# Retention and a leaky-ReLU MLP on one core: half of the loads of blocks 2 to 11 on SyncE's queue, and a new order of the opening

## The chip, the cores and the metric

The kernel runs on one core of a Trainium2 chip. A core has five engines, each with its own in-order instruction queue: TensorE (PE, matrix products; its weight loads are listed as PEld), VectorE (DVE), ScalarE (ACT), GpSimd (POOL) and SyncE (SP). Here GpSimd and SyncE only issue DMA transfers. The metric is device time in microseconds; the time before is the median of three runs.

## The reference

Per batch and head, retention with a decay that depends on the head, then a two-layer MLP over all heads together:

```
scores = q k^T / sqrt(64);  ret = (scores * Dmat) v      # Dmat[i, j] = gamma_h^(i-j) for i >= j, else 0
x      = ret, heads side by side                         # 4608 tokens x 512
out    = leaky_relu(x @ w_in, 0.01) @ w_out              # w_in 512 x 2048, w_out 2048 x 512
```

q, k and v are 8 batches x 8 heads x 576 tokens x 64, float32; inside, the kernel computes in fp16 with float32 sums.

## The kernel before

**Blocks and groups.** The 4608 tokens are 36 blocks of 128 (two chunks of 64), four blocks make a group of 512 tokens. Per block the retention part runs, with the decay folded into q, k and v and a running state per head; the MLP runs per group. Its first layer is plain for groups 0 and 1; from group 2 on, and for all second layers, it is a seven-product scheme (Strassen-like) with sums on VectorE.

**Jobs.** Each piece of work is a job with a name, and one string, `ORDER`, lists all jobs in the sequence in which they are emitted. So each engine's queue holds its jobs in the sequence of that string, and waits (semaphores) follow from the data. A table `ENGINE` says which of VectorE and ScalarE does a job that either could do. `CFG["loads"]` says which queue issues each load. The jobs that matter here, for block u and group g:

| job | engine | what it does |
|---|---|---|
| `ldu.0`, `ldu.1`, `ldu.2` | POOL or SP | load q, k, v of block u, 256 KB each, into a float32 buffer t_0, t_1 or t_2; there are four buffers of each (128 KB halves where a block spans two batches) |
| `cqu`, `cku`, `cvu` | DVE or ACT | cast q, k, v to fp16 (q and v scaled); this frees the load's buffer |
| `tpu.x`, `ytu.x` | PE, DVE/ACT | transpose q (x=0) or k (x=1) on TensorE (line 411) and copy the result; from block 8 on `tru`, a DMA transpose on SyncE |
| `sbu` | PE | state products k^T v (line 454); needs cku and cvu |
| `stu.j`, `sxu` | DVE, ACT | add the state of chunk j (lines 485 to 491), cast it |
| `sau`, `mku` | PE, DVE | scores and mask (lines 445, 460) |
| `oau` or `cau`, `owu`; `xu` | PE; ACT/DVE | output products (line 542), copy into xT |
| `wif`, `woc` | POOL | load a quarter of w_in, w_out, cast to fp16 on the way |
| `hg.f.t`, `lg.f.t` | PE, ACT | plain first layer: feature tile f, tokens from t (line 640), and its leaky ReLU |
| `+n` | PE | n idle matrix products (filler, line 980) while TensorE has no data |

h0.4 to h0.7 need w_in quarter 1, h0.8 to h0.11 quarter 2, h0.12 to h0.15 quarter 3, h0.0 to h0.3 quarter 0. In the text, q3, k3, v3 stand for the loads of block 3, wi1 for w_in quarter 1.

The load itself and where a state product gets its waits:

```
def run(t=t, x=x, c=c, parts=parts, eng=eng):          # line 346
    for j, rows in parts:
        b, w = (c + j) // CB, (c + j) % CB
        engine[eng].dma_start(
            out=t[CH * j : CH * j + rows],
            in_=(q, k, v)[x][b, :, CH * w : CH * w + rows, :].rearrange("h t d -> t h d"),
        )
...
jb = add(
    f"sb{u}", "PE", sb, [cast[u, 1], cast[u, 2]] + states.get(u - 1, []), [], [qk16[u], v16[u], sc_banks],
    mode="q",
)
```

**What sets the order around the change.** Three things: each queue is issued in its own sequence; a load waits until the cast that last read its buffer is done; and each queue has eight semaphore lanes used in turn, so a DMA also waits until the eighth before it on the same kind of queue (GpSimd's, or SyncE's and ScalarE's together) has landed. Buffers are given out in the sequence in which loads appear in `ORDER`.

Of the kernel before, what the change touches and what calls it, by code (L numbers as in the profile page):

```python
# [33 lines left out]
class Plan:  # L34
# [52 lines left out]
    for eng, names in {  # L87
        "DVE": """
            ck0 cq0 sx0.0 yt0.0 cq1 sx0.1 cv1 cq2 sx1.0 yt2.1 ck3 cq3 yt3.1 cv3 sx2.1 yt3.0 cq4 cv4 x3 ck5 cq5
            cv5 yt5.1 cq6 sx5 cv6 cq7 ck7 cv7 yt7.0 b0.cA cv8 ck10 sx8.0 cv9 cq9 cq11 cq12 cv10 b1.cA cv13 ck15  # L90
            cv14 cq14 cv15 cq15 sx13.1 sx14 cq16 cv16 cv17 cq17 cq18 a2.3.k5 sx17.0 cv18 sx18 cq19 a3.1.u2 x17
            cv20 ck21 cq21 sx19 a3.2.k5 cq22 cv22 sx20 ck23 cv23 cq23 x20 cv24 cq25 sx23 a4.2.cA cv25 a4.2.u2
            cq26 cq27 cv27 sx25 a5.0.u2 a5.0.k5 cq28 cq29 cv29 ck30 cq30 cv30 ck31 cv31 cq32 sx30 cq33 ck33
            a6.0.cA cv33 cv34 ck34 cq35 cq34 a6.2.cA b5.u2 cv35 a6.3.u2 x32 a7.0.cA x33 a7.0.k5 b5.21 a7.1.cA
            b6.11 b6.u2 a7.3.cA a7.3.u2 a8.0.k5 b7.k5 a8.2.u2 a8.2.k5 b7.21 a8.3.u2 b8.21
        """,
        "ACT": """
            cv0 yt0.1 x0 ck1 ck2 yt1.1 yt1.0 cv2 yt2.0 x1 sx1.1 sx2.0 x2 sx3.0 ck4 sx3.1 yt4.1 yt4.0 ck6 sx4.1
            x4 yt5.0 x5 yt6.0 yt6.1 sx6 yt7.1 sx7 x7 x6 ck8 b0.11 cq8 ck9 b0.u2 cq10 b0.k5 cv11 ck12 sx9 x8 ck11
            cv12 sx10 cq13 b0.21 x9 ck13 sx11 b1.11 sx12 x10 b1.u2 x11 ck14 a2.0.cA b1.k5 a2.0.u2 a2.0.k5 x12  # L100
            a2.1.cA a2.1.u2 x13 a2.1.k5 ck16 ck17 sx15 a2.2.cA a2.2.u2 b1.21 a2.2.k5 sx16 x14 a2.3.cA x15
            a2.3.u2 ck18 b2.cA a3.0.cA b2.11 a3.0.u2 a3.0.k5 a3.1.cA cv19 b2.u2 x16 a3.1.k5 ck19 b2.k5 a3.2.cA
            ck20 cq20 a3.2.u2 cv21 b2.21 ck22 x18 a3.3.cA a3.3.u2 a3.3.k5 x19 b3.cA a4.0.cA b3.11 sx21 ck24
            a4.0.u2 a4.0.k5 cq24 a4.1.cA a4.1.u2 sx22.1 a4.1.k5 x21 b3.u2 ck25 b3.k5 ck26 sx24 a4.2.k5 x22 cv26
            a4.3.cA x23 a4.3.u2 a4.3.k5 ck27 b3.21 a5.0.cA b4.cA ck28 cv28 sx26.0 b4.11 x24 ck29 a5.1.cA a5.1.u2
            a5.1.k5 x25 sx27 sx28 b4.u2 a5.2.cA x26 sx29 b4.k5 a5.2.u2 a5.2.k5 x27 a5.3.cA ck32 a5.3.u2 cv32
            a5.3.k5 cq31 b4.21 x28 x29 sx31.1 a6.0.u2 a6.0.k5 sx32 b5.cA a6.1.cA b5.11 a6.1.u2 x30 a6.1.k5 x31
            a6.2.u2 a6.2.k5 sx33 b5.k5 ck35 a6.3.cA a6.3.k5 sx34 sx35.0 a7.0.u2 b6.cA a7.1.u2 a7.1.k5 a7.2.cA
            a7.2.u2 b6.k5 a7.2.k5 x34 x35 a7.3.k5 a8.0.cA b6.21 a8.0.u2 b7.cA b7.11 a8.1.cA b7.u2 a8.1.k5
            a8.1.u2 a8.2.cA a8.3.cA a8.3.k5 b8.cA b8.u2 b8.k5 b8.11x so8.11x b8.11y  # L110
# [7 lines left out]
    yt0.1 ld3.1 st0.0 ck1 yt0.0 ld3.0 cq2 yt1.0 tp1.1@3 ck2 sa0 +3@1 cv1 ld4.1 yt1.1 st0.1 sx0.0 sb1 tp2.1@2 +2@0
    mk0 ld3.2 sx0.1 cv2 sa1 tp2.0@1 ld4.0 st1.0 oa0 +7@0 mk1 sx1.0 st1.1s x0 yt2.1 yt2.0 sx1.1 sa2 sb2 oa1 +2@0
    ld5.0 x1 ck3 wi2 st2.0 tp3.1@0 mk2 h0.6.0@3 +2@1 ld4.2 st2.1 ck4 cq3 l0.6.0 yt3.1 tp3.0@2 ld5.1 sx2.0 h0.4.0@1  # L120
    yt3.0 cv3 ld5.2 sa3 oa2 cq4 sb3 wi3 x2 tp4.1@3 st3.0 mk3 l0.4.0 wi0 h0.4.256@0 sx3.0 sx2.1 cq5 ld6.0 oa3
    l0.4.256 tp4.0@2 x3 tp5.0@1 yt4.0 st3.1s ld6.1 h0.11.0@0 sx3.1 yt5.0 ld6.2 h0.9.0@2 yt4.1 ck5 cv4 ld7.0
    h0.10.0@1 l0.9.0 tp5.1@3 ld7.2 l0.10.0 ca4 sb4 h0.4.384@2 mk4 ld7.1 cv5 h0.8.0@1 l0.4.384 st4.1 ld8.2 yt5.1 ow4
    sb5 x4 h0.15.0@2 st5.0 sx4.1 st5.1 l0.11.0 h0.14.0@3 sx5 ld8.1 ca5 l0.14.0 cq6 l0.8.0 ld9.2 ws3.1 h0.13.0@0 mk5
    ld9.1 h0.0.128@3 l0.13.0 cv6 wo2 h0.0.384@1 l0.0.128 ld10.2 l0.15.0 tp6.0@0 h0.0.256@3 ck6 yt6.0 ld10.1 tp6.1@2
    l0.0.384 ow5 sb6 wo0 x5 h0.12.0@0 st6.0s yt6.1 ld8.0 h1.0.0@1 cv7 l0.0.256 cq7 ld9.0 h1.2.0@2 l1.0.0 ck7 st6.1
    ld10.0 tp7.0@3 h1.8.0@1 yt7.0 wo1 m0.0.0 h1.12.0@3 l1.8.0 ws3.0 sx6 ck8 ca6 sb7 l1.12.0 ld11.2 h0.0.0@1 st7.0
    l1.2.0 cv8 ck9 h1.4.0@3 mk6 ld12.2 l0.12.0 st7.1 h1.14.0@2 l0.0.0 cv9 wo3 l1.4.0 m0.1.0 tp7.1@0 sx7 sb8 h1.6.0@1
    st8.0s yt7.1 ow6 ca7 h1.10.0@3 ld11.1 x6 mk7 l1.14.0 wm2.0 ow7 sb9 ld13.2 m0.2.0 x7 b0.p1.0@0 l1.6.0 wm0.0
    h1.12.256@2 l1.10.0 cv10 ld11.0 wm1.0 h1.2.256@1 m0.0.1 h1.8.256@3 l1.2.256 m0.1.1 ld14.2 l1.12.256 h1.14.256@1  # L130
    sx8.0 l1.8.256 st9.0 ck10 b0.p1.1 l1.14.256 ws1.1 cq8 m0.2.1 h1.10.256@2 b0.cA@3 h1.0.256@1 ws1.0 b0.p6.0 st9.1
# [920 lines left out]
```

## Time and profile before

| | |
|---|---|
| median of three runs (lowest, highest) | 280.47 us (278.8, 280.89) |
| the profiled execution: its time, its span | 279.54 us, 277.7 us |
| granted TensorE clock, mean | 0.999 |
| busy: PE, DVE, ACT, POOL | 268.1, 229.8, 206.7, 72.4 us |
| chain that ended last | PE 91%, DMA 5% (loads of k), others 1% each or less |
| moved by DMA | 50.04 MB, mean 180 GB/s |
| loads on GpSimd's queue | 32 of v, 10 of q, 10 of k (256 KB), and halves |
| loads on SyncE's queue | 22 of q, 22 of k (256 KB), and halves |

The page lists busy time by engine, the chain of work followed back from the last instruction, groups of instructions by source line, and the DMA queues (q0 is GpSimd's, q1 SyncE's). A time behind a DMA row is that from issue to landing. All times are from the start of the span unless they are called the time of a run. The idle products count as busy, so TensorE's 97% is not all useful work.

### The profile page before, as it was taken

The numbers are of one execution on the slowest core, as the hardware profiler recorded it, in microseconds if no ns is written. First come the engines' busy times: TensorE is split into PE (matmuls) and PEld (weight loads), VectorE is DVE, ScalarE is ACT, GpSimd is POOL, SyncE is SP. The second block draws the span as 40 slices with busy tenths as digits, with TensorE's granted clock in tenths as the row PEclk, the third lists the DMA queues.
The fourth block names the chain that finished last, engine by engine and source line by source line (L and its number), as shares of the span: only waits on it lengthen the run. The fifth ranks groups of instructions, "written<-read, shape, count | busy, mean of one in ns | idle before, by whom it ended". The sixth has DMA issues, their size and how long they took to land.

```text
span 277.7 us, 10117 instructions
## 1 busy us (share of the span) xinstructions
PE 268.1 (97%) x4337; PEld 224.4 (81%) x4337; DVE 229.8 (83%) x431; ACT 206.7 (74%) x459; POOL 72.4 (26%) x92
## 2 busy tenths in 40 slices
...
GB/s 219 224 240 238 293 287 269 277 216 177 208 256 220 220 295 227 173 236 230 257 222 255 183 228 183 170 247 219 20 139 74 44 2 2 153 0 0 78 97 132
DMA packets 94364, 50.04 MB, mean 180 GB/s; under 512 B 83312, under 2 KB 88560, under 8 KB 94320
## 3 DMA queue, kind: packets, MB, share of 16 engines
...
q0 software_dynamic: 11264, 27.79, 36.1%
...
HBM read 36.81 MB, written 9.44 MB: 167 GB/s over the span
## 4 chain that ended last, share of the span: by engine, by line
PE 91%; DMA 5%; POOL 1%; ACT 1%; issue 1%; DVE 1%; POOLq 0%
PE acc L911 39%; PE acc L833 32%; PE acc L640 10%; DMA t<-in_k_dram 5%; PE ot L542 5%; PE sc L454 2%; PE sc L445 2%; PE sc L911 1%; POOL t L346 1%; PE acc L411 1%; DVE s L487 0%; POOL w_in L612 0%; ACT st L503 0%; DVE qk L375 0%; DVE s L460 0%
## 5 line engine op out<-in xcount | busy, mean ns | idle before, releaser
L911 PEld LDWEIGHTS <-gt 128*128 128x128 f16 x720 | 69.8, 98 | 8.4
L346 POOL DMA_DIRECT2D t<-in_v_dram x40 | 34.2, 857 | 100.5 <-DVE v L375 64.0
L911 PE MATMUL acc<-w_out,gt 128*128 128x256 f16 x416 | 51.5, 273 | 0.0
L833 PEld LDWEIGHTS <-w_in 128*128 128x128 f16 x448 | 42.4, 98 | 5.6
L853 ACT ACTIVATE gt<-acc 128x512 f16<-128x512 f32 x56 | 33.4, 599 | 16.6 <-PE acc L833 16.4
L861 ACT ACTIVATE gt<-sum 128x512 f16<-128x512 f32 x56 | 34.8, 633 | 4.7 <-DVE sum L857 4.7
L911 PE MATMUL acc<-w_mix,gt 128*128 128x256 f16 x288 | 36.2, 273 | 0.0
L833 PEld LDWEIGHTS <-w_sum 128*128 128x128 f16 x336 | 32.2, 98 | 4.1
L833 PE MATMUL acc<-xs,w_sum 128*128 128x256 f16 x224 | 33.6, 273 | 0.0
L833 PE MATMUL acc<-xT,w_in 128*128 128x256 f16 x224 | 33.5, 273 | 0.0
L833 PE MATMUL acc<-xs,w_in 128*128 128x256 f16 x224 | 33.4, 273 | 0.0
L730 POOL DMA_DIRECT2D out_dram<-osb x16 | 11.5, 718 | 83.9 <-ACT acc L772 38.5
L640 PE MATMUL acc<-xT,w_in 128*128 128x256 f16 (+2 forms) x272 | 30.8, 266 | 0.7 <-ACT qkT L418 0.4
L911 PEld LDWEIGHTS <-mix 128*128 128x128 f16 x288 | 28.1, 98 | 3.3
L460 DVE TENSOR_TENSOR s<-sc,cs 128x512 f16<-128x512 f32 x36 | 24.6, 684 | 4.4 <-PE sc L445 2.3
L640 PEld LDWEIGHTS <-w_in 128*128 128x128 f16 x272 | 22.0, 98 | 5.8 <-issue 0.9
L857 DVE TENSOR_TENSOR sum<-acc,k 128x512 f32<-128x512 f32 x28 | 19.2, 686 | 7.9 <-PE acc L833 5.7
L647 ACT ACTIVATE gt<-acc 128x512 f16<-128x512 f32 x32 | 18.2, 601 | 6.3 <-PE acc L640 6.2
L786 ACT COPY k<-acc 128x512 f32<-128x512 f32 x29 | 17.0, 588 | 7.5 <-PE acc L833 3.7
L375 DVE TENSOR_TENSOR qk<-t,cs 128x512 f16<-128x512 f32 x30 | 20.5, 684 | 2.3 <-DMA t<-in_q_dram 2.3
L591 ACT CAST xT<-ot 128x512 f16<-128x512 f32 x31 | 18.2, 588 | 4.6 <-PE ot L542 4.6
L381 ACT ACTIVATE v<-t,cs 128x64 f16<-128x64 f32 x72 | 18.3, 343 | 4.1 <-DMA t<-in_v_dram 3.4
...
## 6 DMA issues: line engine op xcount, KB each, us to landing
t<-in_v_dram POOLq DMA_DIRECT2D x32, 256.0 KB, 5.1
out_dram<-osb POOLq DMA_DIRECT2D x16, 512.0 KB, 4.5
t<-in_k_dram SPq DMA_DIRECT2D x22, 256.0 KB, 4.8
t<-in_q_dram SPq DMA_DIRECT2D x22, 256.0 KB, 5.0
t<-in_q_dram POOLq DMA_DIRECT2D x10, 256.0 KB, 8.5
t<-in_k_dram POOLq DMA_DIRECT2D x10, 256.0 KB, 6.5
w_in<-in_moe_w_in_dram POOLq DMA_DIRECT2D x4, 512.0 KB, 7.8
w_out<-in_moe_w_out_dram POOLq DMA_DIRECT2D x4, 512.0 KB, 9.7
```

Of the source, the lines that this page charges most:

```text
L346: engine[eng].dma_start(out=t[CH * j : CH * j + rows], in_=(q, k, v)[x][b, :, CH * w : CH * w + rows, :].rearrange("h t d -> t h d"),)
L375: engine[e].tensor_tensor(out=view[0](out), in0=view[1](t32[u, 2 * x][:]), in1=view[1](decay(u, x)), op=MUL)
L381: nc.scalar.mul(out=out[:, at(h), :], in_=t32[u, 2 * x][:, h, :], mul=tab_sb[:, w, x, h : h + 1])
L460: landed[u] = nc.vector.tensor_tensor(out=s[:], in0=sc[:, :, 0], in1=mask_sb.unsqueeze(1).unsqueeze(1).to_broadcast([P, 2, NP, CH]), op=MUL,)
L591: moved[u] = copies[xe](out=x_of(u).rearrange("q c (j t) -> q j c t", j=2), in_=at)
L640: nc.tensor.matmul(out=a[:, n, :], lhsT=w_in16[:, c, (f0 + n) * P : (f0 + n + 1) * P], rhs=x[:, c, t0 : t0 + nt], start=(n == 0 and c == 0 ...
L647: nc.scalar.activation(out=y[:, f0 : f0 + nf, t0 : t0 + nt], in_=a[:], func=mybir.ActivationFunctionType.Lrelu)
L833: nc.tensor.matmul(out=r[:, f, :], lhsT=w[:, c, (2 * n + f) * P : (2 * n + f + 1) * P], rhs=rhs[:, c, :], start=fresh and c == 0 and f == ...
L853: w = op(what, "ACT", lambda: nc.scalar.activation(out=to(), in_=r[:], func=lr), after, [y], [r])
L857: what, "DVE", lambda: nc.vector.tensor_tensor(out=s[:], in0=r[:], in1=plus[:], op=ADD),
L861: f"l{g}.{n}.{what}", "ACT", lambda: nc.scalar.activation(out=to(), in_=s[:], func=lr), [j], [y],
L911: nc.tensor.matmul(out=(r[tb] if isinstance(r, tuple) else r)[:, tb, :], lhsT=lhs[n]()[:, f, tb * P : (tb + 1) * P], rhs=rhs[n][:, f, :], ...
```

## The change

Before, SyncE issues only k and q of block 0 in the opening and GpSimd everything else up to block 11. After, SyncE issues 15 of the 30 loads of blocks 2 to 11; k and q of block 3 and k of block 4 stand ahead of the first w_in quarter on GpSimd's queue; and the jobs of the opening stand in a new sequence, up to about group 1's second layer, with some casts and copies on another engine and 29 fillers instead of 33. From the middle of `ORDER` on nothing differs. Each triple names the queues for k, q and v.

```
-        ("u", 0, ("SP", "SP", "POOL")), ("wi", 0), ("u", 1, "POOL"), ("u", 2, "POOL"), ("wi", 1), ("u", 3, "POOL"),
-        ("wi", 2), ("u", 4, "POOL"), ("wi", 3), ("u", 5, "POOL"), ("u", 6, "POOL"), ("u", 7, "POOL"), ("wo", 0),
-        ("wo", 1), ("wo", 2), ("wo", 3), ("u", 8, "POOL"), ("u", 9, "POOL"), ("u", 10, "POOL"), ("u", 11, "POOL"),
+        ("u", 0, ("SP", "SP", "POOL")), ("wi", 0), ("u", 1, "POOL"), ("u", 2, ("SP", "SP", "POOL")), ("wi", 1),
+        ("u", 3, ("POOL", "POOL", "SP")), ("wi", 2), ("u", 4, ("POOL", "SP", "SP")), ("wi", 3),
+        ("u", 5, ("SP", "POOL", "SP")), ("u", 6, ("SP", "POOL", "SP")), ("u", 7, ("POOL", "SP", "SP")), ("wo", 0),
+        ("wo", 1), ("wo", 2), ("wo", 3), ("u", 8, ("SP", "SP", "POOL")), ("u", 9, ("SP", "POOL", "POOL")),
+        ("u", 10, "POOL"), ("u", 11, ("SP", "POOL", "POOL")), ("u", 12, ("SP", "SP", "POOL")),
...
 ORDER = """
-    ld0.1 ld0.2 ld0.0 ld1.0 ld1.1 ld2.1 ck0 ld2.0 cq0 ld1.2 cv0 cq1 ld2.2 +13@3 tp1.0@0 wi1 tp0.0@1 tp0.1@2 sb0 +4@3
...
+    ld0.2 ld1.0 ld2.0 cq2 ld0.0 cq0 +10@3 tp2.0@0 cv0 ld1.2 ld0.1 ck0 ld1.1 +3@3 tp0.0@3 +2@1 sb0 cq1 ld2.1 ld2.2
+    ld3.1 ld3.0 ld4.1 st0.0 cv1 wi1 yt2.0 tp0.1@0 st0.1 sx0.0 yt0.0 wi2 tp1.0@1 ck1 +3@2 sb1 ck2 tp1.1@2 yt0.1 yt1.1
...
+    h0.4.0@1 st3.1s h0.6.0@3 ld9.0 l0.4.0 sx3.1 l0.6.0 ld5.1 h0.4.256@2 cv4 wo3 ld5.2 h0.11.0@1 sb4 ck5 yt4.0
+    l0.11.0 ca4 cv5 st4.1 sx4.1 cq5 h0.10.0@3 l0.4.256 l0.10.0 h0.9.0@1 sb5 ld6.1 st5.0 tp5.1@3 l0.9.0 h0.15.0@0
+    h0.14.0@1 mk4 yt5.1 cq6 st5.1 l0.15.0 tp6.0@2 ck7 sx5 ck6 tp5.0@3 h0.8.0@0 yt5.0 h0.12.0@3 ow4 ld6.2 ca5 l0.8.0
```

Three places of the queues follow. In their rows t_0, t_1 and t_2 are buffers of q, k and v, and a wait on DMASW or DMAHW with a number is one for the landing of a transfer of that lane of GpSimd's or of SyncE's and ScalarE's queues.

SyncE's queue at the start of the program before; the third row is the DMA transpose of block 8, and what follows are loads of block 12:

```order
L346 DMA t_1_135<-in_k_dram 128x8x64
L346 DMA t_0_139<-in_q_dram 128x8x64
L397 DMA_TRANSPOSE qkT<-qk_1048 128x8x128 [waits DVE_49,PE_49,Activation_49]
L346 DMA t_1_1417<-in_k_dram 128x8x64 [waits DMASW6_49,DMAHW1_49,DMASW3_49,DMASW2_49]
L346 DMA t_0_1429<-in_q_dram 128x8x64 [waits DMAHW3_49,DMASW5_49,DVE_49]
```

The same place after: q2, q0, k0, k2, v3, the halves of q4 and of v4, k5, v5, k6 and v6.

```order
L352 DMA t_0_139<-in_q_dram 128x8x64
L352 DMA t_0_143<-in_q_dram 128x8x64
L352 DMA t_1_167<-in_k_dram 128x8x64
L352 DMA t_1_202<-in_k_dram 128x8x64
L352 DMA t_2_289<-in_v_dram 128x8x64 [waits DMASW0_49,DVE_49]
L352 DMA t_0_471<-in_q_dram 64x8x64 [waits DMASW1_49,DVE_49]
L352 DMA t_0_471<-in_q_dram 64x8x64 [waits DMAHW0_49]
L352 DMA t_2_474<-in_v_dram 64x8x64 [waits DMAHW1_49,DMASW4_49,DVE_49]
L352 DMA t_2_474<-in_v_dram 64x8x64 [waits DMAHW2_49]
L352 DMA t_1_629<-in_k_dram 128x8x64 [waits DMAHW3_49,DMASW5_49,Activation_49]
L352 DMA t_2_651<-in_v_dram 128x8x64 [waits DMAHW6_49,DMAHW4_49,DVE_49]
L352 DMA t_1_725<-in_k_dram 128x8x64 [waits DMASW7_49,DMAHW5_49,DMASW0_49,Activation_49]
```

Eleven loads now stand on SyncE's queue ahead of anything of block 7, and v4 waits for the buffer of v2 (lane DMASW4 and VectorE's cast), v5 for that of v3 (DMAHW6). v6, the next row, waits for v4's lanes DMAHW1 and DMAHW2 and its cast.

GpSimd's queue before, from the eighth DMA on: wi1, k3, q3, the halves of k4, v3, the halves of q4, q5, wi2:

```order
L612 DMA w_in_122<-in_moe_w_in_dram 128x4x512
L346 DMA t_1_220<-in_k_dram 128x8x64 [waits DMASW0_49]
L346 DMA t_0_226<-in_q_dram 128x8x64 [waits DMASW1_49]
L346 DMA t_1_260<-in_k_dram 64x8x64 [waits DMAHW1_49,DMASW2_49,DVE_49]
L346 DMA t_1_260<-in_k_dram 64x8x64 [waits DMASW3_49]
L346 DMA t_2_293<-in_v_dram 128x8x64 [waits DMASW4_49]
L346 DMA t_0_326<-in_q_dram 64x8x64 [waits DMAHW3_49,DMASW5_49,DVE_49]
L346 DMA t_0_326<-in_q_dram 64x8x64 [waits DMASW6_49]
L346 DMA t_0_445<-in_q_dram 128x8x64 [waits DMASW7_49,DVE_49]
L612 DMA w_in_122<-in_moe_w_in_dram 128x4x512 [waits DMASW0_49]
```

After, from the sixth DMA on: k3, q3, the halves of k4, wi1, wi2, q5, wi3, q6, k7, v9, wi0:

```order
L352 DMA t_1_206<-in_k_dram 128x8x64
L352 DMA t_0_208<-in_q_dram 128x8x64
L352 DMA t_1_210<-in_k_dram 64x8x64 [waits DMAHW4_49,DVE_49]
L352 DMA t_1_210<-in_k_dram 64x8x64 [waits DMASW0_49]
L618 DMA w_in_122<-in_moe_w_in_dram 128x4x512 [waits DMASW1_49]
L618 DMA w_in_122<-in_moe_w_in_dram 128x4x512 [waits DMASW2_49]
L352 DMA t_0_273<-in_q_dram 128x8x64 [waits DMAHW2_49,DMASW3_49]
L618 DMA w_in_122<-in_moe_w_in_dram 128x4x512 [waits DMASW4_49]
L352 DMA t_0_276<-in_q_dram 128x8x64 [waits DMAHW3_49,DMASW5_49]
L352 DMA t_1_283<-in_k_dram 128x8x64 [waits DMASW6_49,Activation_49]
L352 DMA t_2_285<-in_v_dram 128x8x64 [waits DMASW7_49]
L618 DMA w_in_122<-in_moe_w_in_dram 128x4x512 [waits DMASW0_49]
```

k3 and q3 moved ahead of wi1, wi2 moved up by six places, and v9 takes a buffer of v ahead of v4 to v8. Behind these rows come k10, v8, wo2, wo0, wo1, q10, q9, wo3.

VectorE's queue before, around blocks 4 and 5: cv4, mk4, cv5, then st4.1 and the copy of a transpose of block 5:

```order
L375 TENSOR_TENSOR v_678<-t_2_472,cs 128x512 [waits DMASW2_49,DMASW1_49]
L460 TENSOR_TENSOR s_741<-sc,cs 128x512 [waits PE_49]
L375 TENSOR_TENSOR v_745<-t_2_504,cs 128x512 [waits DMASW4_49]
L485 COPY s_753<-sc 128x256
L418 COPY qkT<-acc 128x512
```

After, cv4, cv5, st4.1, its cast, cq5:

```order
L381 TENSOR_TENSOR v_648<-t_2_474,cs 128x512 [waits DMAHW2_49,DMAHW1_49]
L381 TENSOR_TENSOR v_690<-t_2_651,cs 128x512 [waits DMAHW4_49]
L491 COPY s_692<-sc 128x256 [waits PE_49]
L512 CAST st_694<-s_692 128x256 [waits DVE_49]
L381 TENSOR_TENSOR qk_666<-t_0_273,cs 128x2x4x64 [waits DMASW3_49]
```

cv4 and cv5 now follow each other, both wait for loads of SyncE's queue, and mk4 moved behind block 5's first state. On TensorE's queue sb4 stood behind h0.11, h0.9, h0.10, block 5's transposes and ca4; it now stands right behind h0.11, and ca4, h0.10, h0.9 and sb5 follow it.

More of the change, by code (lines that the diff above doesn't have):

```diff
@@ L88 @@
         "DVE": """
[L89 to L93, printed above, removed]
```

93 lines of the change are left out of this document (47 added, 46 removed), and 12 rows, old and new, of the table loads.

## Prediction

> **What bounds the kernel now.** I read the windows first, cutting the span where the fillers end and where the opening's loads end.
>
> ```profile
> core 0: us, PE busy (x), PEclk, DMA share, GB/s
> 0.00:25.30 25.30, 19.41 (x357) 1.00 0.93 232
> 25.30:60.00 34.70, 34.55 (x559) 1.00 1.11 266
> 60.00:277.70 217.70, 214.15 (x3424) 1.00 0.70 161
> ...
> 0.00:25.30 25.30, 9.69 (x33) 3.11 (x33) 1.00 0.93 232
> ```
>
> The last row counts line 980 alone, the fillers. From 25.3 us on TensorE is busy 99% of the time at full clock, so the product work sets the end. The change can win only in the first 25.3 us (9.7 us of fillers and 5.9 us of idle), and it loses whatever new gap it makes, since no later slack gives it back. The same windows show the DMA engines full up to 60 us. The change doesn't alter what must be loaded in that stretch, only the sequence.
>
> The chain of waits and TensorE's timeline say what the opening waits for.
>
> ```profile
> 8.31 8.90 DMA t<-in_k_dram
> ...
> 17.97 0.40 PE L411 MATMUL acc<-ident,qk 128*128 128x128 f16 x4 [1.33 <-DVE qk L371]
> 25.30 2.75 PE L640 MATMUL acc<-xT,w_in 128*128 128x512 f16 x12 [0.41 <-ACT qkT L418]
> 28.42 0.29 PE L454 MATMUL sc<-v,qk 64*64 64x64 f16 x8
> 30.69 0.32 PE L454 MATMUL sc<-v,qk 64*64 64x64 f16 x14
> 37.39 0.30 PE L454 MATMUL sc<-v,qk 64*64 64x64 f16 x16
> ```
>
> k of block 3 is issued at 8.31 behind the first w_in quarter and lands at 17.21; its transpose follows at 17.97. At 25.30 h0.11, h0.9 and h0.10 start (about 0.9 us each). The last three rows are sb4, sb5 (its last 14 of 16) and sb6, the state products of blocks 4, 5 and 6; I use them as milestones.
>
> **What the new order wins.** k3 and q3 now stand before every w_in quarter on GpSimd's queue, which issues one load per 0.9 us, and SyncE issues four loads beside it in some 0.5 us each. The costs of moving data come from the traffic rows of four windows (5 to 9.5, 124.5 to 126.5, 26 to 29 and 10 to 13 us).
>
> ```profile
> DMA packets 462, 1.51 MB, mean 335 GB/s; under 512 B 94, under 2 KB 94, under 8 KB 462
> DMA packets 2280, 0.58 MB, mean 288 GB/s; under 512 B 2280, under 2 KB 2280, under 8 KB 2280
> DMA packets 616, 0.63 MB, mean 210 GB/s; under 512 B 18, under 2 KB 614, under 8 KB 615
> DMA packets 385, 0.41 MB, mean 137 GB/s; under 512 B 12, under 2 KB 376, under 8 KB 385
> ```
>
> A 256 KB load (0.262 MB) takes 0.78 us of the engines from GpSimd's queue (335 GB/s) and 0.91 from SyncE's (288), whose packets are of 256 B: 15 moved loads add 15 x 0.13 = 2.0 us of transfer. A weight quarter (0.524 MB) takes 2.5 us, the first one 3.8 (137 GB/s); I take 2.5 and keep 1.3 for the range.
>
> **In which sequence two queues are served** decides everything else. The opening of before has next to nothing on SyncE's queue, but later stretches have both. The queries at 95 us show this:
>
> ```profile
> out_dram<-osb POOLq DMA_DIRECT2D x1, 512.0 KB, 5.1
> t<-in_v_dram POOLq DMA_DIRECT2D x1, 256.0 KB, 4.6
> t<-in_k_dram SPq DMA_DIRECT2D x1, 256.0 KB, 7.7
> ...
> 93.90 2.31 SPq L346 DMA_DIRECT2D t<-in_k_dram  x2
> 96.25 3.76 SPq L346 DMA_DIRECT2D t<-in_q_dram  x2
> ...
> 94.18 0.89 POOL L346 DMA_DIRECT2D t<-in_v_dram  x1 [3.42 <-DVE v L375]
> 95.06 0.71 POOL L730 DMA_DIRECT2D out_dram<-osb  x1
> ...
> q0 software_dynamic: 134, 0.48, 101.9%
> q1 hardware_dynamic: 34, 0.01, 3.0%
> ```
>
> SyncE's k (issued 94.53, done issuing 96.2) lands at 102.2, behind GpSimd's v (issued 94.18, lands 98.8) and the store (95.06, lands 100.2), though it alone needs 0.9 us. While it waits, from 97.5 to 98.75 (last two rows), GpSimd's queue q0 moves 0.48 MB and SyncE's q1 0.01. So a transfer is served in the sequence in which issues end, over both queues; SyncE's queue is no fast lane past GpSimd's backlog. The row at 96.25 shows a second thing: with two loads outstanding SyncE's next issue itself waits (two issues in 3.76 us instead of 1.0).
>
> **The sum.** I line up the issues by their waits (the order's rows) and serve them in that sequence, in us of landing. The anchors are before's own first transfers: SyncE's first two loads land 3.2 and 4.1 us after issue (0.74 and 1.25), GpSimd's first 4.8 after 1.28.
>
> ```profile
> t<-in_k_dram SPq DMA_DIRECT2D x1, 256.0 KB, 3.2
> t<-in_q_dram SPq DMA_DIRECT2D x1, 256.0 KB, 4.1
> t<-in_v_dram POOLq DMA_DIRECT2D x1, 256.0 KB, 4.8
> ```
>
> That gives q2 3.9, q0 5.4, v0 6.1; then adding 0.78 or 0.91 each: k0 7.0, q1 7.8, v1 8.6, k2 9.5, k1 10.3, v2 11.0, k3 11.8, v3 12.7, q3 13.5, k4 14.3, q4 15.2, wi1 17.7, wi2 20.2. So h0.11 can start at about 20.6 after h0.4, h0.6 and h0.4.256, instead of 25.3: about 4.5 us ahead, as TensorE has then left out only one transpose group (0.2).
>
> Now what is late next. v4 goes into v2's buffer, so SyncE waits for cv2, which stands behind st1.1s on VectorE, till some 13 us. Until then GpSimd has issued wi1, wi2, q5, wi3 (a lane is free as soon as the load eight before has landed: v2 at 11.0) and q6. So v4 is served behind them: q5 21.0, wi3 23.5, q6 24.3, **v4 25.2**. sb4 stands right behind h0.11 and needs cv4 (0.69, the duration of such a row below): TensorE waits from 21.5 to 25.9. Before, sb4 began at 28.42 with h0.9, h0.10, block 5's transposes and ca4 already done (1.8 + 0.5 + 0.45 = 2.75 us), so the same progress was reached at 25.7. The lead is gone: delay 0.2 us.
>
> ```profile
> 26.25 0.69 DVE L375 TENSOR_TENSOR v<-t,cs 128x512 f16<-128x512 f32 x1
> ...
> 31.08 0.89 DVE L487 TENSOR_TENSOR s<-sc,s 128x256 f32<-128x256 f32 x2 [0.37 <-PE sc L454]
> ```
>
> v5 goes into v3's buffer and is issued at about 16, behind k5, k7, v9 and wi0: 26.1, 26.9, 27.7, 30.2, **v5 31.1**. On VectorE cv5 stands ahead of st4.1, and sb5 needs both: 31.1 + 0.6 + 0.4 = 32.1. Before's same progress (sb5 at 30.69, with h0.4.384, h0.8, ow4 and block 5's transposes beyond it, 2.8 us) was at 27.9: delay 4.2.
>
> v6 goes into v4's buffer, so it is issued only after cv4 at 25.9. By then GpSimd has issued k10, v8, wo2, wo0 and wo1, as each of them waits only for its lane (w quarters, q5, q6, landed by 24.3) or for buffers free long before. Behind v5: k6 32.0, k10 32.8, v8 33.6, wo2 36.1, wo0 38.6, wo1 41.1, **v6 42.0**, cv6 and sb6 at 42.7. Before, sb6 ran at 37.39 with five of h0.13, h0.0.x and h0.4.384 (4.5), a transpose (0.2) and ow5 (0.4) more and h0.12 (0.9) less: same progress at 33.2. **Delay 9.5 us**, each milestone counted whole, not added. Up to v7 and block 8 TensorE has enough left to do (5 us up to sb7), so I add nothing.
>
> The four fillers fewer (33 to 29) stand where TensorE waits anyway: nothing. Casts of v that move from ScalarE (8 instructions) to VectorE (one) are hidden by waits for loads. The order from the second group on is the same, so the delay stays.
>
> Both ends: the slow first quarter adds 1.3, and SyncE's blocked issue (at most two loads outstanding, so v5 is issued only when v4 moves, after wo2 and wo0) moves v5 and v6 some 4 us later: up to +15. If only v4 and v5 are late, +4.2. The profiled run took 279.54 us for its span of 277.7, 0.9 below the median of 280.47. I go by the run: 279.54 + 9.5 = **289.0 us**.
>
> **A rule weighed.** The rows of 97.5 to 98.75 show 134 packets of q0 against 34 of q1. The Trainium skill (DMA: Bandwidth & Descriptors, "Queues, rings and completion order") says that each DMA engine takes turns between queues, one packet each. By that rule the counts would be near one to one wherever both have work; this trace agrees only in that the small packets get little. It gives a rival of its own, below.
>
> **The rivals.**
> (a) *Turns by packet.* A SyncE load has 1024 packets of 256 B, 64 per DMA engine; GpSimd's seven opening loads bring about 28 large ones per engine (448 of 4 KB). k0 would then finish only when those run out, near 11.5 instead of 7.0; ck0 holds cq1 and cv1 behind it on VectorE and k4's buffer on GpSimd, so 4.5 us come on top: 293.5. For it: the starved q1. Against: SyncE's k beat nothing that was issued earlier, and nothing later beat it.
> (b) *SyncE's loads get an even share.* This is the other side: then v4, v5 and v6 land within 4 us of issue and never hold TensorE, wi2 slips by two loads to 22.0, and h0.11 starts about 2.8 ahead; the quarters behind give some of it back: -2.2, **277.3 us**. It decides as soon as a SyncE load issued behind three or more GpSimd transfers lands first. For it: no stretch of before has a backlog of six or more GpSimd transfers with SyncE loads behind. Against: the rows at 95 us.
> (c) *Only v4 is late.* If buffers or lanes hold GpSimd back, so that v5 and v6 pass the quarters, the lead of 4.5 and the wait of 4.4 cancel: 279.7, no change.
>
> **How the numbers follow.** My case 0.58 (283.7 with v6 hidden to 294.5; likeliest 289.0), (a) 0.12, (b) 0.17, (c) 0.13. About 1% is what a measurement here can tell from no change. Faster is (b), same is (c), slower the rest: 0.17, 0.13, 0.70. The range 278 to 296 takes in (c) and my case and most of (a), and leaves out most of (b) and a tail above.
>
> **What would show it.** k3's transposes (line 417 now) should run near 13 us, fillers' end should come earlier, and h0.11 near 21. Then TensorE's timeline should show gaps ahead of sb4, sb5 and sb6 that VectorE's v casts end, and those casts should wait for loads of v; SyncE's loads of v4 to v6 should take 10 us and more from issue to landing, GpSimd's w quarters less than now. If those SyncE loads land in 3 to 5 us, the service rule is wrong and (b) holds. If TensorE is dense from 21 us on, my sum of the waits is wrong.

## The result and the profile after

The changed kernel takes 296.45 us (median of 4 runs, 295.98 to 297.48) against 279.85 before: 1.060 times as long, interval 1.055 to 1.065. The prediction said 289.0 and slower; the direction held, and the loss is 16.6 us instead of 9.5. Its profiled run took 296.52 us for a span of 294.7, 17.0 more than before. (The profiles of two experiments below, k6_pool and pool_4to11b, show an execution somewhat longer than most of their kernel, so only waits, landings and packet counts are read from them.)

The windows of the kernel after, TensorE alone, the first three cut as before:

```profile
core 0: us, PE busy (x), PEclk, DMA share, GB/s
0.00:25.30 25.30, 19.99 (x348) 0.93 1.07 249
25.30:60.00 34.70, 23.11 (x357) 0.75 1.07 225
60.00:294.70 234.70, 230.89 (x3656) 1.00 0.69 153
...
20.00:27.00 7.00, 6.71 (x84) 0.80 1.15 262
27.00:35.00 8.00, 0.03 (x3) 0.66 1.18 230
35.00:42.00 7.00, 4.50 (x46) 0.50 1.21 211
42.00:50.00 8.00, 7.07 (x81) 0.71 1.09 226
50.00:62.00 12.00, 12.00 (x291) 1.00 0.99 193
```

Between 25.3 and 60 us TensorE is busy 23.1 of 34.7 us, where it was 34.55 before, and part of that at half clock. From 50 us on it is dense again, as before. TensorE's timeline names the gaps; the bracket holds the idle time ahead of a group and what ended it.

```profile
14.56 0.40 PE L417 MATMUL acc<-ident,qk 128*128 128x128 f16 x4
...
22.34 0.58 PE L417 MATMUL acc<-ident,qk 128*128 128x128 f16 x4
22.74 3.79 PE L646 MATMUL acc<-xT,w_in 128*128 128x256 f16 x36
26.70 0.31 PE L460 MATMUL sc<-v,qk 64*64 64x64 f16 x8 [0.18 <-DVE v L381]
34.99 0.26 PE L548 MATMUL ot<-qkT,st 64*64 64x64 f16 x2 [7.97 <-ACT qkT L424]
35.45 3.60 PE L646 MATMUL acc<-xT,w_in 128*128 128x512 f16 x8
41.55 0.43 PE L460 MATMUL sc<-v,qk 64*64 64x64 f16 x16 [2.50 <-DVE s L491]
...
49.93 0.32 PE L460 MATMUL sc<-v,qk 64*64 64x64 f16 x16 [0.94 <-DVE v L381]
```

The rows at 26.70, 41.55 and 49.93 are sb4, sb5 and sb6. Before's same progress at sb6 was 33.2, so sb6 is late by 16.7 us, which is the whole loss of span (17.0). Most of it is there at sb5: before's same progress at sb4 and sb5 was 25.7 and 27.9, so sb4 is 1.0 us late and sb5 13.7. At sb6 TensorE itself waits only 0.94 us for the cast of v6; the other 2 us come with dense work at a clock of 0.71. The gap of 8 us ends with the copy of block 4's q; ahead of that copy ScalarE holds the cast of k5, which waits for its load. The casts ahead of sb4 to sb6, and that of k5, all wait for loads on SyncE:

```profile
25.96 0.69 DVE L381 TENSOR_TENSOR v<-t,cs 128x512 f16<-128x512 f32 x1 [1.95 <-DMA t<-in_v_dram]
40.47 0.69 DVE L381 TENSOR_TENSOR v<-t,cs 128x512 f16<-128x512 f32 x1 [13.82 <-DMA t<-in_v_dram]
49.19 1.29 DVE L381 TENSOR_TENSOR v<-t,cs 128x512 f16<-128x512 f32 x2 [1.95 <-DMA t<-in_v_dram]
...
33.84 0.62 ACT L377 CAST qk<-t 128x512 f16<-128x512 f32 x1 [8.54 <-DMA t<-in_k_dram]
```

So SyncE's loads land v4 25.9, k5 near 33.8, v5 40.4, k6 47.6, v6 49.2: 8, 7 and 7 us apart, then, once GpSimd's queue is empty, 1.5. The traffic of 33 to 40 us, where both queues have work all the time, says why (packets, MB, share of the engines; q0 is GpSimd's queue, q1 SyncE's).

```profile
q0 software_dynamic: 1102, 1.09, 91.9%
q1 hardware_dynamic: 1101, 0.28, 30.0%
```

SyncE's timeline shows its issues blocked meanwhile (start, us; a free one takes 0.5 us).

```profile
16.34 5.54 SPq L352 DMA_DIRECT2D t<-in_v_dram  x1
22.05 8.06 SPq L352 DMA_DIRECT2D t<-in_k_dram  x1
```

The two queues move the same number of packets, 157 per us each, though GpSimd's average 1 KB and SyncE's are 256 B. A SyncE load has 1024 of them, so it needs 1024 / 157 = 6.5 us of turns. From 18 to 45 us the counts are 3876 to 3877, and in each single microsecond of that stretch they differ by 5 at most. So SyncE's queue always had packets to move there, and the blocked issues did not hold it up. With GpSimd's queue empty it moved 942 packets in one microsecond (49 to 50).

Turns of one packet each are the rule of the Trainium skill that the prediction weighed (DMA: Bandwidth & Descriptors, "Queues, rings and completion order"); here the trace agrees with it, 1102 to 1101.

### The profile page after: what moved, and what is told of

Read it like the earlier page. It is cut to its first block, busy times and chain, and to the rows that moved or that the text cites. A ratio compares the mean times of both kernels' runs of the same rounds, so it can differ in the third digit from the quotient of the medians.

```text
span 294.7 us, 10091 instructions
## 1 busy us (share of the span) xinstructions
PE 274.0 (93%) x4333; PEld 226.7 (77%) x4333; DVE 230.7 (78%) x431; ACT 202.2 (69%) x438; POOL 58.2 (20%) x75
## 4 chain that ended last, share of the span: by engine, by line
PE 79%; DMA 12%; SPq 3%; DVE 2%; ACT 2%; issue 1%; POOL 0%; DVEq 0%
PE acc L917 33%; PE acc L839 30%; PE acc L646 6%; DMA t<-in_v_dram 6%; PE ot L548 4%; DMA t<-in_k_dram 4%; SPq L352 3%; PE sc L460 2%; DMA t<-in_q_dram 2%; PE sc L451 1%; PE sc L917 1%; PE acc L986 1%; ACT xT L597 1%; DVE v L381 0%; DVE mix L893 0%
## 5 line engine op out<-in xcount | busy, mean ns | idle before, releaser
L352 POOL DMA_DIRECT2D t<-in_v_dram x34 | 29.4, 866 | 127.7 <-DVE v L381 104.1
L839 PEld LDWEIGHTS <-w_in 128*128 128x128 f16 x448 | 42.4, 98 | 5.9 <-DVE xs L819 0.3
L859 ACT ACTIVATE gt<-acc 128x512 f16<-128x512 f32 x56 | 33.4, 600 | 16.7 <-PE acc L839 16.5
L867 ACT ACTIVATE gt<-sum 128x512 f16<-128x512 f32 x56 | 34.7, 633 | 4.7 <-DVE sum L863 4.7
L917 PE MATMUL acc<-w_mix,gt 128*128 128x256 f16 x288 | 36.4, 273 | 0.0
L381 DVE TENSOR_TENSOR v<-t,cs 128x512 f16<-128x512 f32 x29 | 19.7, 683 | 18.8 <-DMA t<-in_v_dram 17.9
L646 PE MATMUL acc<-xT,w_in 128*128 128x256 f16 (+2 forms) x272 | 34.3, 281 | 0.0
L839 PE MATMUL acc<-xT,w_in 128*128 128x256 f16 x224 | 33.5, 273 | 0.0
L736 POOL DMA_DIRECT2D out_dram<-osb x16 | 11.5, 719 | 83.8 <-ACT acc L778 39.0
L646 PEld LDWEIGHTS <-w_in 128*128 128x128 f16 x272 | 22.9, 101 | 6.4 <-issue 3.3
L377 ACT CAST qk<-t 128x512 f16<-128x512 f32 x25 | 15.6, 622 | 14.9 <-DMA t<-in_k_dram 14.9
L381 DVE TENSOR_TENSOR qk<-t,cs 128x512 f16<-128x512 f32 x31 | 21.1, 682 | 5.7 <-DMA t<-in_q_dram 2.9
L597 ACT CAST xT<-ot 128x512 f16<-128x512 f32 x29 | 17.1, 589 | 7.4 <-PE ot L548 5.2
```

Source lines behind the costliest of these rows:

```text
L352: engine[eng].dma_start(out=t[CH * j : CH * j + rows], in_=(q, k, v)[x][b, :, CH * w : CH * w + rows, :].rearrange("h t d -> t h d"),)
L377: copies[ke](out=by_half(t[:, 1]), in_=in_halves(t32[u, 1][:]))
L381: engine[e].tensor_tensor(out=view[0](out), in0=view[1](t32[u, 2 * x][:]), in1=view[1](decay(u, x)), op=MUL)
L597: moved[u] = copies[xe](out=x_of(u).rearrange("q c (j t) -> q j c t", j=2), in_=at)
L646: nc.tensor.matmul(out=a[:, n, :], lhsT=w_in16[:, c, (f0 + n) * P : (f0 + n + 1) * P], rhs=x[:, c, t0 : t0 + nt], start=(n == 0 and c == 0 ...
L839: nc.tensor.matmul(out=r[:, f, :], lhsT=w[:, c, (2 * n + f) * P : (2 * n + f + 1) * P], rhs=rhs[:, c, :], start=fresh and c == 0 and f == ...
```

## The experiments

**Theory T (turns):** while GpSimd's queue has a backlog, the queues go packet for packet, so whatever stands on SyncE's queue is served at its packets' pace. **S (sequence):** the prediction's rule, transfers are served in the sequence in which issues end. **O (order):** the new order of the work loses time by itself. **C (clock):** the low clock of 27 to 50 us costs. Of the nine times that T gave in what follows, only the last was met; its landings did better.

### loads_only: the queues changed, the work not

```diff
 (the table "loads" of the change in the kernel before, its ORDER untouched)
-("u", 2, "POOL"), ("wi", 1), ("u", 3, "POOL"), ("wi", 2), ("u", 4, "POOL"),
+("u", 2, ("SP", "SP", "POOL")), ("wi", 1), ("u", 3, ("POOL", "POOL", "SP")), ("wi", 2), ("u", 4, ("POOL", "SP", "SP")),
...
```

> The kernel before with the changed kernel's queues for the loads and nothing else: before's order of the work. Theory T (turns: both queues move packet for packet while both have a backlog, so a SyncE load of 1024 packets needs about 7 us of turns whatever it is queued behind): SyncE's v5 and v6 land at 38 us or later here too, sb6 is late by 8 us or more, time 288 to 297. Theory S (service in the sequence of issues, as the prediction had it): v6 behind what GpSimd issued before it, 286 to 290. Theory O (the new order costs, with block 5's casts ahead of what ca4 needs, and the queues do not): within 2 us of before, 278 to 282.

Measured: 286.35 us, ratio 1.024 (1.017 to 1.030), just under T's range and against O. TensorE's timeline, with the wait of oa3, sb4 and sb6, and VectorE's cast of q4:

```profile
28.54 0.43 PE L548 MATMUL ot<-s,v 64*64 64x64 f16 x16 [2.82 <-DVE s L466]
34.23 0.29 PE L460 MATMUL sc<-v,qk 64*64 64x64 f16 x8
43.20 0.30 PE L460 MATMUL sc<-v,qk 64*64 64x64 f16 x16
...
26.86 0.69 DVE L381 TENSOR_TENSOR qk<-t,cs 128x512 f16<-128x512 f32 x1 [3.51 <-DMA t<-in_q_dram]
```

sb6 comes in the same sequence of work as before's at 37.39: 5.8 us late, and the span is 6.1 longer. The move of queues alone makes sb6 late; O alone can't explain that. But v5 and v6, which T had named, hold nothing here: sb4, at 28.42 before, is 5.8 us late already, and no wait follows. The time goes ahead of that, in the opening, and the largest wait of 20 to 30 us is for q4: SyncE issued its second half at 8.2, it landed at 26.9, and behind its cast on VectorE stands the mask that oa3 needs. S's range (286 to 290) holds the time, but the traffic speaks for turns: from 12 to 27 us the queues moved 2135 and 2137 packets. GpSimd's queue ran dry near 28 us here, so v5 and v6 came in time; in the changed kernel it lasted to 46.

### long_runs and runs_512: the same bytes in fewer packets

```diff
+if eng == "SP" and 2 <= u <= 11:      # long_runs: one 2 KB run per partition
+    src = (q, k, v)[x][b].rearrange("h (s r) d -> (h s) (r d)", r=H)[CH * j : CH * j + rows]...
...
+    src = (q, k, v)[x][b, 0:4].rearrange("f (s r) d -> s f (r d)", r=2)[...]   # runs_512: four of 512 B
```

> The changed kernel, but SyncE's loads of blocks 2 to 11 read one run of 2 KB per partition in place of eight of 256 B: the same bytes, queue, buffers and waits, 128 packets in place of 1024. The data of these blocks are then other parts of q, k and v, so the output differs; every operation runs as before. Theory T (turns by packet): a load needs 8 times fewer turns, so SyncE's v4, v5 and v6 land within 3 to 5 us of issue, the waits ahead of sb5 and sb6 go, time 279 to 285. Theory S (service in the sequence of issues): the packets only save 0.13 us a load, 15 x 0.13 = 2 us, time 293 to 295. If what costs is the issue on SyncE's queue (descriptors per load, not turns on the engines), both may fall together: then the issue of v5, 5.5 us, falls to under 1 us too, and turns and issue are not told apart.

> As the kernel with runs of 2 KB, but with runs of 512 B: SyncE's loads of blocks 2 to 11 take 512 packets, half of the changed kernel's 1024 and four times the 128 of the other; the data of these blocks are again other parts of q, k and v, so the output differs. Theory T: the time of v5, k6 and v6 in the backlog goes with their packets, so sb6 starts between 35.6 (2 KB runs) and 49.9 us (256 B), nearer the first, at 37 to 41; the whole time 284 to 291. If only packets under 512 B are slow, sb6 comes at 35.6 as with 2 KB; if the packets' number did not matter, at 49.9.

Measured: 290.24 us with runs of 2 KB (ratio 1.037, 1.029 to 1.045) and 293.46 with 512 B (1.051, 1.044 to 1.058). TensorE's timeline of long_runs, with sb6 and the longest wait, and its traffic of 33 to 40 us:

```profile
35.59 0.34 PE L462 MATMUL sc<-v,qk 64*64 64x64 f16 x16
...
59.79 0.32 PE L550 MATMUL ot<-qkT,st 64*64 64x64 f16 x6 [6.46 <-DMA qkT<-qk]
```

```profile
q0 software_dynamic: 873, 0.92, 74.9%
q1 hardware_dynamic: 520, 0.94, 40.5%
```

The same of runs_512, sb6 and the traffic:

```profile
39.89 0.43 PE L462 MATMUL sc<-v,qk 64*64 64x64 f16 x16 [2.42 <-DVE v L383]
```

```profile
q0 software_dynamic: 993, 1.05, 84.3%
q1 hardware_dynamic: 996, 0.49, 34.4%
```

sb6 starts at 35.6, 39.9 and 49.9 us for 128, 512 and 1024 packets per load, with the same bytes, queue, buffers and waits. With 512 packets the counts are again equal (993 to 996) and SyncE's bytes are 0.49 MB instead of 0.28; with 128 SyncE no longer has work all the time. S, which gave 0.13 us a load, is out. In long_runs SyncE's issues shrink too (0.33 us each): the blocked issue goes with the packets. The time fell by only 6 us and 3 us, and T's ranges (279 to 285 and 284 to 291) missed both, since new waits came: in long_runs the row at 59.79 waits 6.5 us for block 8's transpose, a DMA on SyncE issued at 45.1; in runs_512 TensorE waits 3.4 us, to 51.8, for the cast of a q load of SyncE's. The loads that land earlier only bring TensorE to the next transfer that GpSimd's backlog holds up.

### warm: the clock kept up

```diff
-    l0.11.0 ca4 cv5 st4.1 sx4.1 cq5 h0.10.0@3 l0.4.256 l0.10.0 h0.9.0@1 sb5 ...
+    l0.11.0 +32@3 ca4 cv5 st4.1 sx4.1 cq5 h0.10.0@3 l0.4.256 l0.10.0 h0.9.0@1 +9@3 sb5 ...
```

> The changed kernel with 41 idle products more, 32 ahead of ca4 and 9 ahead of sb5, where TensorE waits with nothing to do (27 to 35 and 39 to 41.5 us), so that its granted clock need not fall (0.66, 0.50 and 0.71 in 27 to 50 us). If v6's landing at 49.2 sets the end, nothing is won: sb6 starts at 50 as before, 296 (295.5 to 297). If the low clock costs time, the products from 35 to 50 us go at full speed and 3 to 4 us come back: 292 to 293.

Measured: 297.23 us, ratio 1.063 (1.057 to 1.069): nothing won. Two of its windows, and sb6 in TensorE's timeline:

```profile
27.00:35.00 8.00, 8.00 (x61) 0.99 1.18 229
35.00:42.00 7.00, 6.41 (x48) 1.00 1.21 210
```

```profile
49.86 0.32 PE L460 MATMUL sc<-v,qk 64*64 64x64 f16 x16 [1.73 <-DVE v L381]
```

At full clock from 27 us on TensorE is ready for sb6 at 48.1 instead of 49.0 and waits that much longer for v6; sb6 starts at 49.86. C is out as a term of its own: the low clock comes with the gaps, and as long as v6 lands at 49 the time it takes is hidden in the wait for it.

### Taking the late loads out of the way, one group at a time

wo_late:

```diff
-    ... oa0 wo2 +1@2 ... tp3.0@0 wo0 yt3.1 x0 wo1 ... cv4 wo3 ld5.2
+    ... ld10.2 wo2 wo0 wo1 wo3 st6.0s          # GpSimd's v10 waits for v6's buffer
```

> The changed kernel with the four w_out quarters moved on GpSimd's queue behind v10, whose buffer v6 frees, so that they are issued only when v6 is cast; SyncE's loads stay where they are. Theory T (turns by packet): SyncE's loads are slow only while GpSimd's queue has a backlog; without w_out it runs out near 35 us, by when SyncE has had some 1400 of the 3072 packets of v5, k6 and v6, and the rest go in 0.9 us a load: v6 near 37 in place of 49.2, sb6 near 38, 279.5 + 38 - 33.2 = 284.3, range 282 to 287. If SyncE's own issue (5 to 8 us a load) were slow whatever GpSimd does, v6 stays beyond 43 and the time above 290.

Measured: 300.0 us (1.073, 1.068 to 1.078). The time is a miss; the landings are not. v5, k6 and v6 landed at 36.4, 37.3 and 38.2 (0.9 us apart with GpSimd's queue empty, as T said). But k5, still in the backlog, was cast at 35.0 and again held ca4 to 36.1, sb5 started at 40.1, and the work up to sb6 ran at a clock of 0.69 (36 to 46 us), so sb6 came at 45.9 and not near 38. Then the w_out quarters, issued at 46 to 48, landed from 53 to 63, and block 8's transpose on SyncE, issued at 54.9, landed at 68.1. sb6 and ca8:

```profile
45.92 0.34 PE L460 MATMUL sc<-v,qk 64*64 64x64 f16 x16
...
68.17 0.31 PE L548 MATMUL ot<-qkT,st 64*64 64x64 f16 x6 [5.59 <-DMA qkT<-qk]
```

v456k56_pool:

```diff
-("u", 4, ("POOL", "SP", "SP")), ... ("u", 5, ("SP", "POOL", "SP")), ("u", 6, ("SP", "POOL", "SP")),
+("u", 4, ("POOL", "SP", "POOL")), ... ("u", 5, "POOL"), ("u", 6, "POOL"),
+    ... cv2 ld3.2 ld5.0 ld4.2 wi3 ... ld5.1 ... cv3 ld5.2 ... cv4 ld6.1 ld6.2 ld8.2 wo2 wo0 wo1 wo3 ...
```

> The changed kernel with v4, k5, v5, k6 and v6 back on GpSimd's queue, each ahead of what it had to wait for there (v4 behind q5; k5 and v5 behind w_in quarter 0; k6 and v6 behind q9), and w_out behind them; the new order of the work otherwise as it is. Both theories of the queues: these loads land in the sequence of GpSimd's queue, v4 near 22, v5 near 30, v6 near 35, sb6 near 36, 279.5 + 36 - 33.2 = 282.3, range 280 to 285. If the new order of the work itself costs what the change lost, the time stays above 290.

Measured: 295.9 us (1.057, 1.053 to 1.062), again a miss in time, though the waits for k5, v5 and v6 are gone: sb6 at 38.2. By the time alone the run would speak for O; the trace shows the loss at another place. SyncE still had v7, q8 and q7, behind GpSimd's w_out. Its timeline:

```profile
32.98 5.83 SPq L352 DMA_DIRECT2D t<-in_q_dram  x2
```

VectorE's and TensorE's, the casts of q7 and q8 and the transposes that wait for them:

```profile
52.90 1.29 DVE L381 TENSOR_TENSOR qk<-t,cs 128x512 f16<-128x512 f32 x2 [6.96 <-DMA t<-in_q_dram]
53.65 0.61 PE L417 MATMUL acc<-ident,qk 128*128 128x128 f16 x4 [7.44 <-DVE qk L381]
```

v7 landed at 42.4, q8 at 49.0 (6.6 us later, one load's turns) and q7, whose cast comes first, at 52.9.

k6_pool:

```diff
-("u", 6, ("SP", "POOL", "SP")),
+("u", 6, ("POOL", "POOL", "SP")),
+    ... ck4 ld6.1 wo2 tp3.0@0 ...          # ld6.1 out of its place behind sb5
```

> The changed kernel with one load moved: k6 on GpSimd's queue ahead of w_out in place of SyncE's. In the changed kernel SyncE's loads end one after the other, v4 25.9, k5 near 33.8 (the start of its cast), v5 40.5, k6 47.6, v6 49.2, while GpSimd's queue is busy to about 45. Theory T (turns: each SyncE load in the backlog costs the next one about 7 us): one load fewer ahead of v6 brings it to 43 or 44, as GpSimd's backlog ends there, and sb6 to 44.5: 279.5 + 44.5 - 33.2 = 290.8, range 289 to 293. Theory I (v6 is late since its own issue waits for its buffer and for SyncE's queue, not for turns): v6's issue moves by what k6's took, 8 us, and lands 2 to 3 us later, near 33 to 36: 282 to 285. If k6 sets the time only by its own cast, v6 stays at 49 and the time at 296.

Measured: 296.0 us (1.059, 1.055 to 1.063), no gain where T said 5 us. In its profile k5, v5 and v6 landed at 37.6, 44.5 and 49.4, and GpSimd's last w_out quarter at 49.2: v6 again came with the end of GpSimd's backlog. I had that end at 45. The larger error is in what v6 could win: k6 stands behind v5 on SyncE's queue, so v5 and sb5 gain nothing from its move, and in the changed kernel TensorE waits at sb6 for v6 only 0.94 us. No more than that was to be had, and the third case on record, 296, is what came, if for another reason than k6's cast.

pool_4to11:

```diff
+("u", 4, ("POOL", "SP", "POOL")), ("u", 5, "POOL"), ... ("u", 11, "POOL"),
+    ... cv2 ld4.2 ld5.1 ld5.2 wi3 ld5.0 ld6.0 ld6.1 ld6.2 wi0 ... cv3 ld7.0 ld7.1 ld7.2 ... cv4 ld8.2 ld8.1 ... sb4 yt4.0 ck5 ...
```

> The changed kernel's new order of the work with all contested loads back on GpSimd's queue in the sequence of need: of blocks 4 to 11 only q4 stays on SyncE; v4, k5 and v5 stand behind w_in quarter 2, then quarter 3, blocks 5 and 6, quarter 0, blocks 7 to 10 and w_out between them as in the kernel before; k5's cast stands behind the copy that ca4 waits for. Theory T: nothing is starved, the loads land in the sequence of GpSimd's queue, h0.11 starts near 21.5 (quarter 2 near 20.8) and sb4 to sb6 wait at most 1 or 2 us: 277 to 282, so the order of the work is worth at most the lead of 4 us. If the order of the work itself loses time (as against before), it stays above 286.

Measured: 300.3 us (1.076, 1.072 to 1.080). One load, q4, was left on SyncE, and in this order its buffer came free late. It was issued at 16.2, in two halves. Timelines of SyncE, VectorE and TensorE:

```profile
16.20 1.39 SPq L352 DMA_DIRECT2D t<-in_q_dram  x2
...
30.60 0.69 DVE L381 TENSOR_TENSOR qk<-t,cs 128x512 f16<-128x512 f32 x1 [10.85 <-DMA t<-in_q_dram]
...
32.28 0.43 PE L548 MATMUL ot<-s,v 64*64 64x64 f16 x16 [8.70 <-DVE s L466]
```

```profile
q0 software_dynamic: 441, 0.82, 112.5%
...
q0 software_dynamic: 459, 0.51, 92.3%
q1 hardware_dynamic: 456, 0.12, 28.9%
```

The second rows are the traffic of 17 to 20 us (nothing of q1) and of 21 to 24 (one for one). A single load of 256 KB took 14 us, VectorE's queue stood still behind its cast for 10.9, and TensorE waited 8.7; two more waits, of 3.4 and 2.3 us, follow by 85 us. In all the kernel lost 21 us.

### pool_4to11b and pool_4to11c: the new order with nothing contested on SyncE

```diff
-("u", 4, ("POOL", "SP", "POOL")),
+("u", 4, "POOL"),
+    ... ld3.1 ld3.0 ld4.1 ld4.0 ... ld8.2 ld8.1 ld8.0 ... cv8 cv9 ... tp6.1@0 ck7 ...
```

> As the kernel with blocks 4 to 11 on GpSimd's queue, and now q4 too, directly behind k4 and ahead of w_in quarters 1 and 2 (q4, left on SyncE behind the buffers of q5 and q6, was issued at 16.2 there and landed at 30.6, while VectorE waited 10.9 us for it); q8 moved ahead of w_out, and the casts of k7 and v9 behind what blocks 6 and 8 need. Only the opening's loads of blocks 0 to 2 and v3 stay on SyncE, where GpSimd has little queued. Theory T (what cost was SyncE's loads behind GpSimd's backlog, not the new order of the work): quarter 2 near 21, h0.11 near 22, sb4 near 23, sb5 near 26, sb6 near 31 to 33, TensorE without a gap over 2 us, 277 to 281. Theory O (the new order of the work loses time by itself): a gap over 5 us stays ahead of one of these with all its loads landed, and the time is above 285.

Measured: 292.4 us (1.043, 1.037 to 1.050), once more a miss in time of T, with the gaps ahead of sb4 to sb6 gone (28.5, 30.8 and 35.6). TensorE's list of waits from 20 to 62 us (total, times, longest) has the rest, block 8's transpose again, issued on SyncE at 45.3:

```profile
PE ot L548 <- DMA qkT<-qk: 8.8, 1, 8.8
```

pool_4to11c:

```diff
-    ... ow7 ld12.1 h1.10.0@2 ... sb9 m0.1.1 ca8 m0.2.0 ck12 ck10 ...
+    ... tr8 ld12.1 h1.14.0@2 ... h1.4.256@3 st9.1 l1.4.256 ca8 mk8 ... cv11 ck12 ...
```

> As the kernel before it in this study (blocks 4 to 11, q4 too, on GpSimd), where TensorE was without a wait over 0.5 us from 20 to 53 us and then waited 8.8 us for block 8's transpose, a DMA on SyncE's queue that took from 45.3 to 61.5 behind GpSimd's w_out and loads. Now SyncE issues that transpose ahead of the load of k12 (in place of behind it, so 1024 packets fewer ahead of it), and the job that reads it, ca8, stands behind four more tiles of the first layer (3.5 us). Theory T: the wait of 8.8 goes to 0 to 3 us and the time to 283 to 287; what is left over before is the opening (sb6 at 35.6 against before's 33.2) and the last w_out quarter (57). Theory O (the new order loses time by itself, wherever the transfers run): a wait as long comes back elsewhere before 75 us, 290 to 293.

Measured: 283.05 us, ratio 1.011 (1.008 to 1.014), inside T's range. sb6 and ca8 in TensorE's timeline, and one of its windows:

```profile
34.43 0.34 PE L460 MATMUL sc<-v,qk 64*64 64x64 f16 x16
57.76 0.25 PE L548 MATMUL ot<-qkT,st 64*64 64x64 f16 x6 [0.76 <-DMA qkT<-qk]
```

```profile
20.00:27.00 7.00, 6.81 (x115) 0.76 1.11 283
```

With the order of the work kept in its main lines, some 13 of the 16.6 us are back. That is with the moves above, among them k5's cast behind the copy that ca4 needs, so O is bounded and not excluded: what the new order so mended still loses is the 3 us left or so, part of it a low clock in 20 to 27 us. In loads_only the queues alone cost 6.8; that both together cost 16.6 is more than the two, and no run splits the rest. The new order issues more on GpSimd ahead of v6 (k7, v9, k10, v8, three w_out quarters), and its backlog lasted to 46 us instead of 28; that this is the reason is argued and not shown. The transpose still took 13.5 us (44.2 to 57.7); it now only stands behind work that fills the time.

### k3q3_first and open_early: could the opening be had without SyncE?

```diff
 (kernel before)
-... +13@3 tp1.0@0 wi1 ... sb0 +4@3 yt0.1 ld3.1 st0.0 ck1 yt0.0 ld3.0 ...
+... +13@3 tp1.0@0 ld3.1 ld3.0 wi1 ...            # k3q3_first
+... +13@3 tp1.0@0 ld3.1 ld3.0 ld3.2 wi1 wi2 ...  # open_early
```

> The kernel before with the loads of k3 and q3 moved ahead of the second quarter of w_in (wi1) on GpSimd's queue; nothing else, every load stays on its queue. By the sum: k3 and q3 land two quarters' place earlier or about 2.5 us, wi1 2 x 0.78 us later, wi2 as before (24.5), and wi2 is what h0.11 and h0.9 wait for at 25.3, so 279 to 280 (no change). If the transposes of block 3 held TensorE instead, 1 to 2 us are won: 278.

> A version that could beat the kernel before: before with all queues as they are, and on GpSimd's queue k3, q3 and v3 ahead of w_in quarters 1 and 2, both ahead of k4, q4 and q5; the work of blocks 3 and 4 follows that sequence. h0.11 waits in before for quarter 2 (24.5) and x3 (25.1). By the sum, quarter 2 lands at 11.5 + 3 x 0.78 + 4.0 + 2.5 = 20.3 and x3 is done near 22, so h0.11 starts near 22.7 in place of 25.3: 277 us, if the loads of blocks 4 to 7, which come 2.5 us later, don't hold TensorE afterwards. If they do, the lead is given back: 279 to 281.

Measured: 279.7 us (1.001, 0.997 to 1.005) and 280.46 (1.006, 1.002 to 1.010). The first is the no change that was expected. In the second h0.11 started at 24.6, not 22.7, and the lead of 0.7 us was given back. No version tried beats the kernel before.

## Why the prediction was right or wrong

**No slack gives anything back: right.** sb6 was 16.7 us late, the span 17.0 longer.

**The service rule: wrong, and this is the step that failed.** I read from the rows at 95 us that a transfer is served in the sequence in which issues end. The window of 97.5 to 98.75 (134 packets to 34) was too short and too early for that: it ends as SyncE's queue begins to move again. The next stretch of the trace of before, 98.75 to 100, reads

```profile
q1 hardware_dynamic: 838, 0.21, 75.2%
q0 software_dynamic: 47, 0.13, 34.0%
```

while GpSimd's store, whose issue had ended before k's, was still on its way to 100.2. By themselves these counts are no proof of turns, nor against a sequence kept on each DMA engine alone; the changed kernel rules that out too. There the issue of v5 ended at 21.9, and GpSimd's v8 and wo2, issued behind it at 22.3 and 23.2, landed at 33.5 and 36.8, ahead of v5 at 40.4. What I took for waiting in a line was, as far as the runs show, the time from issue to first packet (q4 above: issue ended at 17.6, no packet before 20). The runs put turns in its place: 1102 to 1101, 993 to 996, and sb6 at 35.6, 39.9 and 49.9 by packets per load.

**The sum of the landings.** In the step on v4, v5 and v6 the terms were 25.2, 31.1 and 42.0; measured 25.9, 40.4 and 49.2. v4 was near only because the waits before it were few. By turns the sum is 25.9 + 3 x 6.5 = 45.4 for k5, v5 and k6, and v6 behind them as GpSimd's queue runs out: 46 to 47, a delay of some 14 us and 293 to 294 in all. The 3 us still missing come from loads of 7 to 8 us instead of 6.5: between 24 and 33 us, beside the larger packets of the weight quarters, each queue moved only 99 to 155 packets per us. By milestone I had 0.2, 4.2 and 9.5 us at sb4, sb5 and sb6; measured were 1.0, 13.7 and 16.7, so the landings of k5 and v5 were mis-sized most, and v6 adds little behind them. GpSimd's own quarters slipped by much less (w_in quarter 0 at 31.9 instead of 30.2, the third w_out quarter at 43.4 instead of 41.1). The blocked issue, which I kept for the upper end at +4, was there (5.5 and 8.1 us).

**The gap ahead of ca4: missed.** I let TensorE go on to sb5 after sb4. The 8 us ahead of ca4 came from the order of ScalarE: k5's cast, which I had landing at 26.1, stands ahead of the copy that ca4 needs. sb5 would have waited for k5 and v5 anyway.

**The lead of 4.5 us: wrong.** Quarter 2 landed at 21.6 (20.2 predicted) and k3's transposes ran at 14.6 (near 13), but the products that end with h0.11 began only at 22.74: blocks 2 and 3 still had to go through casts, scores and x3, and the clock was at 0.80. So h0.11 came no earlier than before's 25.3. I had asked only which load is last and not which work. It cost 0.8 us at sb4 (26.7 instead of 25.9), since the sum had already spent the lead on v4's wait.

**The rivals.** (a), turns by packet, had the right mechanism at the wrong place: k0 landed at 8.1, not 11.5, as GpSimd's queue did not yet have work all the time (from 4 to 8 us it moved 33 to 66 packets per us, SyncE's 407 to 778); the price was paid at v5, k6 and v6. I had held the shallow rows of before against it. (b), an even share, fails at its own test: v5, k6 and v6 passed no GpSimd transfer that was issued ahead of them. The share is even in packets, but SyncE moves 0.28 MB beside GpSimd's 1.09. (c), only v4 late, fails with v5 and v6.

**Four fillers fewer and the casts of v.** No run isolates them. The clock was 0.80 in 20 to 27 us, and 1.00 before; whether the four fillers would have kept it up was not tried, so the "nothing" there had no measurement behind it.
